# Seven accumulators of one pool for the main products and the shared work, in the place of four and three

## The chip, the cores and the metric

The kernel runs on one core of a Trainium2 chip. Its time is the device time of one execution in microseconds (us); the figure given for the kernel is the median of several runs. About 0.2% (1.4 us) is what a measurement of this kernel can tell from no change.

## What is computed

Three steps follow each other: attention that is read from a small state in both directions, a gated product (GLU) with a norm in front, and a mixture of experts over 32 soft slots.

```
# x: 8 x 8 x 512 x 64, state: 8 x 8 x 32 x 64
xread = softmax(scale * x @ state.T) @ state          # 512 rows of each batch and head
sread = softmax(scale * state @ x.T) @ x              # 32 rows of each batch and head
x = concat([xread, sread], 2) -> 4608 tokens x 512    # 8 heads x 64 side by side

xn = x / sqrt(mean(x * x) + 1e-6) * rms_g
h = silu(xn @ w_gate) * (xn @ w_val)                  # 512 -> 1536; weights arrive as float64
x = h @ w_out                                         # 1536 -> 512

logits = x @ phi                                      # 32 slots: 8 experts of 4
d = softmax over tokens(logits); c = softmax over slots(logits)
slot_out[e] = relu((d.T @ x)[e] @ w1[e]) @ w2[e]      # 512 -> 1024 -> 512
out = c @ slot_out
```

## The kernel before

A batch's 512 read rows are one group g of four tiles t of 128 tokens; the rows that the state reads form a last, smaller group. d_ff is cut into three chunks c of 512. A **unit** is one (g, c, t). In each unit TensorE (PE) makes the gate product of the tile (six matmuls of 128 x 512 into one accumulator, `mm<-wp,A` in the rows), ScalarE (ACT) takes its silu (L471), PE transposes an earlier unit's h (L109, `misc<-ident,h`), PE makes the value product (six more matmuls), VectorE (DVE) multiplies the two (L479, `h<-mm,rinv,sg`), and the logits of an earlier tile are added up (`lg<-hT,wphi`). Twelve units make a stage of one group.

The weights of the main products are not the raw ones: since attention's read is linear in the state, `sw` first multiplies the state's rows by the gate or value weights of a chunk (`misc<-w,stTg`). One call fills two accumulators, one for each half of the state's partitions (64 of the 128), with eight small matmuls each as the trace counts them; ACT copies each accumulator, rounded (L442), and DVE subtracts that from it for the rest (L443). The plan calls `sw` twice in a row, for gate and value, so four accumulators are filled one after another.

All else on PE goes through the same helper: scores (`misc<-xT,stT`), transposes (`sT`, `a`, `srd`), the product e2T (`misc<-xn,e2T`), the block product `misc<-bd,A`, the slots' inputs (`misc<-h,ET`), and, in the first part, `wphi_part`, which multiplies w_out by phi: per chunk two products `misc<-wo,phis`, gathered by DVE (L632 copy, L635 add, tile `wpp`), then `misc<-r,wpp`.

A plan written by hand says in which unit and slot each of these runs. The framework's scheduler makes from it one fixed instruction order per engine, and may pull a main matmul ahead into a gap where an accumulator is free by its reckoning. An engine runs its own list strictly in order. The accumulators lie in PSUM, which has eight banks of 128 x 512 float32:

- `mmps()` (L79): the main products' tiles, tag `mm`, four buffers. `keep_warm` (L106) and the products at the end take theirs here too.
- `misc()` (L82): all shared tiles, tag `misc`, three buffers.
- one bank for the logits, later for the experts' output (`lg`, `so`).

A tile waits until the tile that held its buffer before has been read for the last time. In `sw` the fourth tile of four takes the bank of the first.

The float64 weights come as bits by SyncE's (SP's) queue and are converted by ACT (L184, L187), DVE (L200, L204, L208) and GpSimd (POOL, L212). At about 97 to 116 us the last ones of the first stages are being made, among them w_out's (`wo`).

Of the kernel before, what the change touches and what calls it, by code (L numbers as in the profile page):

```python
# [8 lines left out]
F32 = mybir.dt.float32  # L9
# [11 lines left out]
def kernel(  # L21
# [17 lines left out]
    B, P, H, NT, D = x_n.shape  # L39
    S = P * NT  # L40
    NS = 32
    DM = H * D
# [10 lines left out]
    big = ctx.enter_context(tc.tile_pool(name="big", bufs=1))  # L53
    psp = ctx.enter_context(tc.tile_pool(name="psp", bufs=1, space=PSUM))
# [20 lines left out]
    def small(name, shape, bufs=1, dt=F32):  # L75
        return sm.tile(shape, dt, tag=name, bufs=bufs, name=name)

    def mmps():
        return psp.tile([P, 512], F32, tag="mm", bufs=4, name="mm")  # L79

    def misc():
        return psp.tile([P, 512], F32, tag="misc", bufs=3, name="misc")  # L82

    def mm(o, lhsT, rhs, start=True, stop=True):
        nc.tensor.matmul(out=o, lhsT=lhsT, rhs=rhs, start=start, stop=stop)  # L85

# [1 line left out]
    ident = small("ident", [P, P])  # L88
    make_identity(nc, ident)
    r32 = small("r32", [P, 32])  # L90
# [5 lines left out]
    rs_magic = small("rs_magic", [P, NT], dt=I32)  # L96
    nc.vector.memset(rs_magic.bitcast(F32), RS_MAGIC)

    # Bits of float64's high word, read as float32: the least and greatest that float32 holds.
    EXP_LO, EXP_HI = 2.0 ** -15, 122879.984375  # L100

    def keep_warm(n):
        """Products that nobody reads, so that a short wait doesn't slow the array's clock."""
        ps = mmps()
        for _ in range(n):
            tc.keep_in_program_order(nc.tensor.matmul(out=ps[:, :P], lhsT=ident, rhs=ident, start=True, stop=True))  # L106
# [1 line left out]
    def transpose(o, i):  # L108
        nc.tensor.transpose(o, i, ident)  # L109

# [1 line left out]
    XN, T = {}, {}  # L112

    def load_xt(b):
# [7 lines left out]
    def load_xn(b):  # L122
# [7 lines left out]
    phis = asmall("phis", [P, 4, NSLOT])  # L130
    nc.scalar.dma_start(out=phis, in_=phi)

# [1 line left out]
    dram = ctx.enter_context(tc.tile_pool(name="dram", bufs=1, space=bass.MemoryType.DRAM))  # L134
    w_out32 = dram.tile([DFF, DM], F32, name="w_out32")
    bits = {
        0: w_gate.bitcast(I32), 1: w_val.bitcast(I32), 2: w_out_t.bitcast(I32),
        3: w_out.bitcast(I32),
    }
# [81 lines left out]
                )  # L221


# [1 line left out]
    def att_g(b):  # L225
        stTg = small("stTg", [P, P], bufs=3)
        ins = nc.gpsimd.tensor_tensor(
# [173 lines left out]
    RINV = {}  # L401

    def rinv_from(g, ss, n):
        """(ss / DM + 1e-6) ** -0.5, by Newton's steps from the halved exponent."""
        y = small("rinv", [P, NT], bufs=3)[:, :n]
        v = small("rv", [P, NT])[:, :n]
        a = small("ra", [P, NT])[:, :n]
        i = small("ri", [P, NT], dt=I32)[:, :n]
        nc.vector.tensor_scalar(
            out=v, in0=ss, scalar1=1.0 / DM, scalar2=1e-6, op0=ALU.mult, op1=ALU.add  # L410
        )
        nc.vector.tensor_scalar(  # L412
            out=i, in0=v.bitcast(I32), scalar1=1, scalar2=-1,
            op0=ALU.logical_shift_right, op1=ALU.bitwise_xor,
        )
        nc.gpsimd.tensor_tensor(out=y.bitcast(I32), in0=i, in1=rs_magic[:, :n], op=ALU.add)  # L416
        for _ in range(3):
            nc.vector.tensor_tensor(out=a, in0=y, in1=y, op=ALU.mult)
            nc.vector.scalar_tensor_tensor(
                out=a, in0=a, scalar=-0.5, in1=v, op0=ALU.mult, op1=ALU.mult  # L420
            )
            nc.vector.scalar_tensor_tensor(
                out=y, in0=a, scalar=1.5, in1=y, op0=ALU.add, op1=ALU.mult
            )
        RINV[g] = y

# [1 line left out]
    WP = {}  # L428

    def sw(b, c, gv):  # L430
# [14 lines left out]
            )  # L445
        WP[b, c, gv] = t

# [1 line left out]
    HH, HT, LGP = {}, {}, {}  # L449
    xsg_t = {}  # L450
    wphi = small("wphi", [P, NF, 32])
# [56 lines left out]
                stop=(c == NC - 1),  # L508
            )

# [1 line left out]
    sacc = small("sacc", [P, 1])  # L512
    mrun = small("mrun", [P, 1])
    Q = {}
# [103 lines left out]
            out=v, in0=v, in1=cs[:, :n].unsqueeze(2).to_broadcast([P, n, 32]), op=ALU.mult  # L618
        )

# [1 line left out]
    wphi_done, WPP = set(), {}  # L622

    def wphi_part(c, j):
        """phi' @ w_out' for half of the d_model rows of a 512-wide chunk; j = 1 ends the chunk."""
        wt = WOT.pop((c, j))
        ps = misc()
        for k in range(2):
            mm(ps[32 * k : 32 * k + 32, :], phis[:, 2 * j + k, :], wt[:, k, :])
        if j == 0:  # L630
            WPP[c] = k2("wpp")
            nc.vector.tensor_copy(WPP[c][:64], ps[:64])  # L632
            return
        wp = WPP.pop(c)
        nc.vector.tensor_tensor(out=wp[:64], in0=ps[:64], in1=wp[:64], op=ALU.add)  # L635
        ps = misc()
        for q in range(4):
            mm(ps[:, 32 * q : 32 * q + 32], wp[:64, q * P : (q + 1) * P], r32[:64])
        nc.vector.tensor_copy(
            wphi[:, 4 * c : 4 * c + 4, :], ps[:, :P].rearrange("p (q s) -> p q s", q=4)  # L640
        )
        wphi_done.add(c)

# [1 line left out]
    def sread_prep():  # L645
        xg = k8("xg").rearrange("p a f -> p (a f)")[:, : 4 * B * NS].rearrange(
            "p (k n) -> p k n", k=4
# [23 lines left out]
    WH = {}  # L671

    def w_split(gv, c):
        """The weights' chunk in two float32r parts."""
        w = W.pop((gv, c))
        h, l = k8("wh", F32R), k8("wl", F32R)
        for k in range(4):
            nc.scalar.copy(h[:, k, :], w[:, k, :])
            nc.vector.tensor_tensor(
                out=l[:, k, :], in0=w[:, k, :], in1=h[:, k, :].bitcast(F32), op=ALU.subtract  # L680
            )
        WH[gv, c] = h, l

# [1 line left out]
    EW = {}  # L685
    loads = []
    for c in range(NC):
# [10 lines left out]
    ew_home, ew_free = {}, []  # L698

    def prefetch(n, home=None):  # L700
        """Start the next n loads, in slots of `big` (home None) or of the experts' pool."""
        for _ in range(n):
            if not loads:
                return
            k = loads.pop()
            if home is None:
                t = k8("ew")
            else:
                t = home.tile([P, 4, 512], F32, tag="ew", bufs=4, name="ew_" + "_".join(map(str, k)))
            if k[0] == "wo":  # L710
                src = w_out32[k[1] * 512 : (k[1] + 1) * 512, :].rearrange("(k p) d -> p k d", p=P)
            elif k[0] == "w1":
                src = w1[k[1], :, k[2] * 512 : (k[2] + 1) * 512].rearrange("(k p) f -> p k f", p=P)
            else:
                src = w2[k[1], k[2] * 512 : (k[2] + 1) * 512, :].rearrange("(k p) d -> p k d", p=P)
            nc.sync.dma_start(out=t, in_=src)
            EW[k], ew_home[k] = t, home
# [6 lines left out]
        while ew_free:  # L724
            prefetch(1, ew_free.pop(0))

# [1 line left out]
    def conv1(n=1):  # L728
        wconv(n)
        if len(to_load) > 6 and (to_load[-1][0] < 2 or len(RAW) < 3):  # L730
# [39 lines left out]
        rinv_from(0, T[0, "ss"], NT)  # L770

    pinned.append(1)
# [1 line left out]
    def rinv(b):  # L774
        rinv_from(b, T[b, "ss"], NT)

# [22 lines left out]
    for s, units in enumerate(stages):  # L799
# [65 lines left out]
            at(16, 1, att_a4, 2)  # L865
        else:
            g = s
            o = 4 if s == 1 else 0  # the first unit's place in the usual twelve
            if s == 1:
                at(0, 1, conv1)  # L870
                at(0, 2, wphi_part, 2, 1)
# [38 lines left out]
        for u, (g, c, t) in enumerate(units):  # L910
# [5 lines left out]
            ps = main_mm(g, c, t, 0)  # L916
# [40 lines left out]
    for u, (c, gv) in enumerate(halves):  # L957
# [3 lines left out]
        for t in range(2):  # L961
            ps = main_mm(gs, c, t, gv)
# [30 lines left out]
        prefetch(PU[u])  # L993
    assert not plan

# [1 line left out]
    h_T(*pend[0])  # L997
    lg_mm(*pend[0])
    post1(gs)
# [21 lines left out]
    for c in range(NC):  # L1021
        ps = mmps()
# [5 lines left out]
    ps = misc()  # L1028
# [27 lines left out]
    ps = misc()  # L1056
    for k in range(4):
        mm(ps[:, 32 * k : 32 * k + 32], sip[:, k * P : (k + 1) * P], r32)
    # each expert's inputs of its own slots, zero in the others'
    for e in range(NE):  # L1060
        es = slice(4 * e, 4 * e + 4)
        nc.vector.tensor_tensor(
# [8 lines left out]
    so_ps = psp.tile([P, 512], F32, tag="lg", bufs=1, name="so")  # L1071
# [7 lines left out]
    HP = {}  # L1079

    def expert_in(p):
        """The first products of two experts: slots of one have zeros in the other."""
        for j in range(2):
            ps = mmps()
            for i in range(2):
                e = 2 * p + i
                wt = take(("w1", e, j))
                for k in range(4):
                    mm(
                        ps[32 * k : 32 * k + 32, :], sinE[e][:, k, :], wt[:, k, :],  # L1090
                        start=(i == 0), stop=(i == 1),
                    )
            HP[p, j] = hp1[:, 2 * (p % 2) + j, :]
            (nc.scalar.copy if j else nc.vector.tensor_copy)(HP[p, j], ps)
# [26 lines left out]
                    )  # L1121

    def out_prep():
        """Group 0's weights of the slots, in two parts, each four times."""
        ch = k8("ch", F32R)[:, 0, :P].rearrange("p (t s) -> p t s", s=32)
        cs = k8("cs")[:, :2, :].rearrange("p i (t q s) -> p i t q s", t=NT, q=4)
        cr = k8("csT", F32R)
        nc.gpsimd.tensor_copy(ch, c_all[:, :NT, :])
        for q in range(4):
            nc.gpsimd.tensor_copy(cs[:, 0, :, q, :], ch.bitcast(F32))  # L1130
            nc.gpsimd.tensor_tensor(
                out=cs[:, 1, :, q, :], in0=c_all[:, :NT, :], in1=ch.bitcast(F32), op=ALU.subtract
            )
        return cs, cr
# [76 lines left out]
    c_turn(1)  # L1211
    expert_out(NPAIR - 1)

    # so_ps still has the four parts of each slot's sum; group 0 takes it as it is
    s4 = k8("s4", F32R)
    s4_h, s4_l = s4[:, 0, :], s4[:, 1, :]
    nc.scalar.copy(s4_h, so_ps)
# [16 lines left out]
    ps = misc()  # L1234
# [4 lines left out]
    so_h, so = so2[:, 0, :], so2[:, 1, :]  # L1239
# [64 lines left out]
```

## Time and profile before

| | |
|---|---|
| time, median of 3 runs | 690.22 us (689.71 to 690.36) |
| span of the profiled execution | 691.4 us |
| PE busy | 640.3 us (93%) |
| VectorE busy | 407.7 us (59%) |
| ScalarE busy | 388.9 us (56%) |
| chain that ended last | PE 75%, DVE 7%, ACT 5% |
| one stage in the middle | 63.8 us (283.8 to 347.6), PE busy 62.25 |

PE is close to always busy, so the page's shares say little; what matters is what PE does in its busy time and which waits stand between. In a timeline a row is a run of like matmuls: start, length, what, how many, and in brackets the idle time ahead of it with what ended it.

### The profile page before, as it was taken

How to read it: one execution, taken by the hardware profiler on the slowest of the kernel's cores; microseconds unless marked ns; L12 is line 12 of the kernel's file. 1: busy time of each engine (PE TensorE's matmuls, PEld its weight loads, DVE VectorE, ACT ScalarE, POOL GpSimd, SP SyncE). 2: the span in 40 equal slices, each digit the busy share in tenths (PEclk: the TensorE clock that was granted, in tenths of full speed). 3: DMA queues.
4: the chain of work that ended last, by engine and by line, in shares of the span. 5: the costliest groups of instructions: out<-in, count | busy, mean ns of one | idle time of the engine just before them, and what ended most of it. 6: DMA issues, size and time to landing. Idle time of an engine off the chain costs nothing.

```text
span 691.4 us, 11529 instructions
## 1 busy us (share of the span) xinstructions
PE 640.3 (93%) x4560; PEld 410.6 (59%) x4560; DVE 407.7 (59%) x852; ACT 388.9 (56%) x632; POOL 129.1 (19%) x158
## 2 busy tenths in 40 slices
PE   6789988999989999999999999999999999999980
PEld 4346646456555766566676658665666676753350
DVE  6979996762687457554835673575455355342160
ACT  5477943754776459546764765496446366311170
POOL 2634554230032101110201021011000000002430
PEclk9799998999999999999999999999999999999995
DMA  9940246031042011203110320020081307999957
GB/s 349 404 193 2 101 152 236 1 129 63 1 156 96 5 47 77 96 5 122 45 53 1 122 92 1 19 105 31 1 309 58 122 1 257 326 334 382 344 186 331
DMA packets 33581, 92.55 MB, mean 134 GB/s; under 512 B 1912, under 2 KB 4088, under 8 KB 30712
## 3 DMA queue, kind: packets, MB, share of 16 engines
q1 hardware_dynamic: 33240, 91.76, 36.3%
q8 instruction: 36, 0.59, 0.4%
q14 instruction: 17, 0.14, 0.1%
q10 hardware_dynamic: 288, 0.07, 0.0%
HBM read 79.76 MB, written 12.06 MB: 133 GB/s over the span
## 4 chain that ended last, share of the span: by engine, by line
PE 75%; DVE 7%; ACT 5%; issue 1%; POOL 0%; DVEq 0%; ACTq 0%
PE mm L85 42%; PE misc L85 17%; PE misc L109 10%; PE lg L85 3%; PE so L85 2%; DVE wp L443 1%; DVE h L479 1%; ACT wp L442 1%; ACT L471 1%; DVE wo L200 1%; ACT sg L471 1%; DVE wo L208 1%; DVE rm L272 1%; ACT sT L285 0%; DVE wo L204 0%
## 5 line engine op out<-in xcount | busy, mean ns | idle before, releaser
L85 PE MATMUL mm<-wp,A 128*128 128x512 f32 x1152 | 304.9, 405 | 0.4 <-DVE h L479 0.4
L85 PEld LDWEIGHTS mm<-wp,A 128*128 128x128 f32 x1152 | 207.3, 189 | 64.1 <-issue 24.5
L479 DVE SCALAR_TENSOR_TENSOR h<-mm,rinv,sg 128x512 f32<-128x512 f32 x102 | 76.1, 747 | 131.1 <-PE mm L85 93.6
L471 ACT ACTIVATE sg<-mm,rinv 128x512 f32<-128x512 f32 x102 | 70.2, 690 | 81.0 <-PE mm L85 78.0
L85 PE MATMUL misc<-w,stTg 64*32 64x512 f32 x768 | 81.7, 618 | 17.6 <-DVE wp L443 7.5
L442 ACT CAST wp<-misc 128x512 fp32r<-128x512 f32 x96 | 51.7, 591 | 65.2 <-PE misc L85 63.1
L443 DVE TENSOR_TENSOR wp<-misc,wp 128x512 fp32r<-128x512 f32 x96 | 61.8, 682 | 26.6 <-ACT wp L442 26.1
L109 PE MATMUL misc<-ident,h 128*128 128x128 f32 x408 | 61.3, 277 | 1.9 <-DVE h L479 0.7
L490 ACT COPY hT<-misc 128x512 f32<-128x512 f32 x86 | 49.2, 580 | 24.6 <-PE misc L109 20.5
L109 PEld LDWEIGHTS misc<-ident,h 128*128 128x128 f32 x408 | 50.1, 142 | 18.2 <-DVE wp L443 3.3
L85 PEld LDWEIGHTS misc<-w,stTg 64*32 64x32 f32 x768 | 15.5, 106 | 67.7 <-issue 22.1
L308 POOL TENSOR_TENSOR a<-a,asum 128x1024 f32<-128x1024 f32 x7 | 13.4, 1917 | 132.4 <-issue 84.8
L471 ACT ACT_TABLE_LOAD x28 | 35.9, 1283 | 3.7 <-PE mm L85 3.2
L416 POOL TENSOR_TENSOR rinv<-ri,rs_magic 128x4 int32<-128x4 int32 (+1 forms) x9 | 1.8, 198 | 173.2 <-DVE ri L412 173.2
L397 ACT ACTIVATE misc<-misc 128x512 f32<-128x512 f32 x32 | 18.7, 585 | 26.9 <-PE misc L85 18.8
L212 POOL TENSOR_TENSOR w<-w,raw 128x512 int32<-128x512 int32 x20 | 28.1, 1418 | 27.6 <-ACT wp L442 7.2
L85 PE MATMUL mm<-wh,xsg 128*128 128x512 f32 x96 | 31.7, 399 | 0.0
L85 PE MATMUL misc<-bd,A 128*128 128x256 f32 x192 | 29.6, 292 | 1.5 <-DVE A L380 1.5
L212 POOL TENSOR_TENSOR wo<-wo,raw 128x512 int32<-128x512 int32 x18 | 24.8, 1387 | 32.7 <-DVE wo L208 23.3
L85 PE MATMUL lg<-hT,wphi 128*32 128x512 f32 (+1 forms) x216 | 27.4, 577 | 1.5 <-ACT hT L490 1.5
L85 PEld LDWEIGHTS misc<-bd,A 128*128 128x128 f32 x192 | 25.5, 191 | 5.1 <-DVE A L380 2.2
L85 PE MATMUL misc<-h,ET 128*32 128x512 f32 x204 | 26.4, 596 | 0.0
(196 smaller groups left out, 831.8 us busy)
## 6 DMA issues: line engine op xcount, KB each, us to landing
ew<-in_w_dram SPq DMA_DIRECT2D x27, 1024.0 KB, 8.1
xT<-in_x_t_dram SPq DMA_DIRECT2D x8, 1024.0 KB, 5.5
xn<-in_x_n_dram SPq DMA_DIRECT2D x8, 1024.0 KB, 7.7
raw<-in_w_val_dram SPq DMA_DIRECT2D x6, 1024.0 KB, 16.6
raw<-in_w_out_dram SPq DMA_DIRECT2D x6, 1024.0 KB, 5.0
out_dram<-ob SPq DMA_DIRECT2D x6, 1024.0 KB, 12.1
ew_w<-in_w_dram SPq DMA_DIRECT2D x5, 1024.0 KB, 10.4
raw<-in_w_gate_dram SPq DMA_DIRECT2D x4, 1024.0 KB, 14.2
```

The costliest lines, as they stand in the source:

```text
L85: nc.tensor.matmul(out=o, lhsT=lhsT, rhs=rhs, start=start, stop=stop)
L109: nc.tensor.transpose(o, i, ident)
L200: nc.vector.tensor_scalar(out=dst[:, h], in0=dst[:, h], scalar1=EXP_LO, scalar2=EXP_HI, op0=ALU.max, op1=ALU.min,)
L208: nc.vector.scalar_tensor_tensor(out=a[:, h], in0=hi[:, h], scalar=-0x40000000, in1=a[:, h], op0=ALU.bitwise_and, op1=ALU.bitwise_or,)
L212: nc.gpsimd.tensor_tensor(out=a[:, h], in0=a[:, h], in1=rnd[:, h], op=ALU.add)
L308: (eng or nc.gpsimd).tensor_tensor(out=a3, in0=a3, in1=asum.unsqueeze(2).to_broadcast([P, 32, 32]), op=ALU.mult)
L397: nc.scalar.activation(out=ps, in_=ps, func=AF.Square, accum_out=T[b, "ss"][:, t : t + 1])
L442: nc.scalar.copy(t[:, r, 0, :], ps)
L443: nc.vector.tensor_tensor(out=t[:, r, 1, :], in0=ps, in1=t[:, r, 0, :].bitcast(F32), op=ALU.subtract)
L471: nc.scalar.activation(out=sg, in_=ps, func=AF.Silu, scale=RINV[g][:, t : t + 1])
L479: nc.vector.scalar_tensor_tensor(out=HH[g, c][:, t, :], in0=ps, scalar=RINV[g][:, t : t + 1], in1=sg, op0=ALU.mult, op1=ALU.mult,)
L490: (nc.vector.tensor_copy if on_dve else nc.scalar.copy)(HT[g, c][:, :, t * P : (t + 1) * P], ps.rearrange("p (q n) -> p q n", q=4))
```

## The change

The two helpers take their tiles from one tag with seven buffers. No instruction is added or taken away; the rest of the diff blanks comments and docstrings.

```diff
     def mmps():
-        return psp.tile([P, 512], F32, tag="mm", bufs=4, name="mm")
+        return psp.tile([P, 512], F32, tag="ps", bufs=7, name="mm")
 
     def misc():
-        return psp.tile([P, 512], F32, tag="misc", bufs=3, name="misc")
+        return psp.tile([P, 512], F32, tag="ps", bufs=7, name="misc")
```

The number of banks is the same, but a tile's buffer is now that of the tile seven allocations earlier, whichever of the two helpers made that. The scheduler's order moves with it. In what follows the counts are those of the program (a matmul of `misc<-w,stTg` or `lg`, in full float32, is two in the trace).

PE in a stage in the middle, around the two calls of `sw` (`w_696` and `w_776` are the gate and value weights, `wp_3112` and `wp_3127` the products' weights that are in use; - is before, + after):

```order
+L85 MATMUL mm<-wp_3127,A_2755 128x512 x6
 L85 MATMUL lg<-hT_3158,wphi 32x512 x4
 L85 MATMUL misc<-w_696,stTg 32x512 x8
 L85 MATMUL misc<-w_776,stTg 32x512 x8
-L109 MATMUL misc<-ident,sT 128x128 x4
-L85 MATMUL mm<-wp_3112,A_2755 128x512
-L109 MATMUL misc<-ident,sT 128x128 x4
-L85 MATMUL mm<-wp_3112,A_2755 128x512 x5
+L109 MATMUL misc<-ident,sT 128x128 x8
+L85 MATMUL mm<-wp_3112,A_2755 128x512 x6
```

The four tiles of `sw` stand together in both; the value product that stood farther ahead now stands right before the logits, and the transposes behind are no longer split by a main matmul.

PE at about 97 to 116 us of the first stages, before (`wp_734` to `wp_906` are main products, `wo_828` and `wo_884` two quarters of w_out, `xn_938` the next batch's rows, loaded just then):

```order
L85 MATMUL mm<-wp_869,A_255 128x512 x6
L85 MATMUL misc<-wo_828,phis 32x512 x2
L85 MATMUL mm<-wp_906,A_255 128x512 x6
L85 MATMUL mm<-wp_869,A_255 128x512 x6
...
L85 MATMUL mm<-wp_869,A_255 128x512 x4
L85 MATMUL misc<-xn_938,e2T 32x64 x32
L85 MATMUL misc<-wo_884,phis 32x512 x2
L85 MATMUL mm<-wp_869,A_255 128x512 x2
L85 MATMUL mm<-wp_906,A_255 128x512 x5
L85 MATMUL misc<-r_75,wpp 128x32 x4
```

The same place after:

```order
L85 MATMUL mm<-wp_734,A_255 128x512 x6
L85 MATMUL mm<-wp_869,A_255 128x512 x6
L85 MATMUL misc<-wo_828,phis 32x512 x2
L85 MATMUL misc<-xn_938,e2T 32x64 x32
L85 MATMUL mm<-wp_906,A_255 128x512 x6
L85 MATMUL misc<-wo_884,phis 32x512 x2
L85 MATMUL misc<-r_75,wpp 128x32 x4
```

From `wp_734` to `misc<-r_75,wpp` there are 53 main matmuls before and 18 after; the other 35 now stand behind that product.

PE where w_out's next chunk is multiplied (about 126 to 131 us), before, and then after:

```order
L85 MATMUL lg<-hT_1048,wphi 32x512 x4
L85 MATMUL misc<-wo_954,phis 32x512 x2
L85 MATMUL mm<-wp_1056,A_456 128x512 x5
L85 MATMUL mm<-wp_1108,A_456 128x512 x4
L85 MATMUL misc<-r_75,wpp 128x32 x4
```

```order
L85 MATMUL lg<-hT_1048,wphi 32x512 x4
L85 MATMUL misc<-wo_954,phis 32x512 x2
L85 MATMUL misc<-r_75,wpp 128x32 x4
L85 MATMUL mm<-wp_869,A_255 128x512 x6
L109 MATMUL misc<-ident,h_817 128x128 x8
```

Nine main matmuls that stood between the products with phi and the one that needs DVE's sum of them are gone from there. The third chunk (`wo_1123`) changes in the same way, with eight.

## Rows read from the trace of the kernel before

**Rows 1.** The page, part 1 (busy, share, instructions) and the granted clock in 40 slices:

```profile
PE 640.3 (93%) x4560; PEld 410.6 (59%) x4560; DVE 407.7 (59%) x852; ACT 388.9 (56%) x632; POOL 129.1 (19%) x158
...
PEclk9799998999999999999999999999999999999995
```

**Rows 2.** Who PE waited for: us in total, times, longest:

```profile
PE misc L85 <- DVE wp L443: 7.9, 14, 0.6
...
PE misc L85 <- DVE e2T L318: 3.1, 1, 3.1
```

**Rows 3.** Timeline of PE, one stage in the middle: start, length, work, count, idle ahead:

```profile
345.08 1.92 PE L85 MATMUL misc<-w,stTg 64*32 64x512 f32 x24
347.57 1.06 PE L85 MATMUL misc<-w,stTg 64*32 64x512 f32 x8 [0.57 <-DVE wp L443]
348.57 0.66 PE L109 MATMUL misc<-ident,sT 128*128 128x128 f32 x4
...
389.60 1.91 PE L85 MATMUL misc<-w,stTg 64*32 64x512 f32 x22
391.44 1.65 PE L85 MATMUL mm<-wp,A 128*128 128x512 f32 x6
```

**Rows 4.** Timelines of DVE and ACT behind the first of these bursts:

```profile
346.83 1.89 DVE L443 TENSOR_TENSOR wp<-misc,wp 128x512 fp32r<-128x512 f32 x3 [1.45 <-ACT wp L442]
...
346.21 1.56 ACT L442 CAST wp<-misc 128x512 fp32r<-128x512 f32 x3 [3.23 <-PE misc L85]
```

**Rows 5.** Timeline of PE, 180 to 204 us, the rows with a wait:

```profile
181.08 0.66 PE L109 MATMUL misc<-ident,h 128*128 128x128 f32 x4 [0.62 <-ACT sT L253]
...
191.52 0.66 PE L109 MATMUL misc<-ident,h 128*128 128x128 f32 x4 [0.55 <-DVE acc L596]
192.95 1.09 PE L109 MATMUL misc<-ident,sT 128*128 128x128 f32 x8 [0.78 <-DVE xsT L350]
```

**Rows 6.** Timeline of PE, 94 to 120 us:

```profile
97.17 4.13 PE L85 MATMUL mm<-wp,A 128*128 128x512 f32 x12
...
102.57 8.02 PE L85 MATMUL mm<-wp,A 128*128 128x512 f32 x34
110.53 1.10 PE L85 MATMUL misc<-xn,e2T 128*32 128x64 f32 x64
111.44 1.03 PE L85 MATMUL misc<-wo,phis 128*32 128x512 f32 x4
112.40 1.89 PE L85 MATMUL mm<-wp,A 128*128 128x512 f32 x7
116.02 1.39 PE L85 MATMUL misc<-r,wpp 64*128 64x32 f32 x8 [1.73 <-DVE wpp L635]
```

**Rows 7.** What this place waits for: SP's issue, its landing time, DVE's sum:

```profile
101.99 0.46 SPq L126 DMA_DIRECT2D xn<-in_x_n_dram  x1
...
DMA to landing us min/median/max: 7.1/7.1/7.1
...
115.29 0.67 DVE L635 TENSOR_TENSOR wpp<-misc,wpp 64x512 f32<-64x512 f32 x1
```

**Rows 8.** Windows: stretch, its length, busy of PE, PEld, DVE, ACT, POOL, clock, DMA share, GB/s:

```profile
116.00:165.00 49.00, 48.82 (x326) 27.65 (x329) 29.50 (x59) 30.27 (x48) 12.13 (x11) 0.93 0.22 79
...
118.00:120.00 2.00, 2.00 (x16) 1.35 (x22) 0.15 (x1) 1.02 (x2) 0.00 (x0) 0.50 0.00 0
...
538.60:595.00 56.40, 56.38 (x298) 41.91 (x299) 29.28 (x55) 32.58 (x56) 0.00 (x0) 1.00 0.43 150
595.00:650.00 55.00, 53.42 (x405) 26.43 (x407) 16.33 (x58) 8.65 (x20) 9.21 (x26) 1.00 1.00 356
```

**Rows 9.** Timeline of PE and DVE where w_out's second chunk is multiplied:

```profile
127.65 2.56 PE L85 MATMUL mm<-wp,A 128*128 128x512 f32 x9
130.31 1.07 PE L85 MATMUL misc<-r,wpp 64*128 64x32 f32 x8
...
129.59 0.67 DVE L635 TENSOR_TENSOR wpp<-misc,wpp 64x512 f32<-64x512 f32 x1
```

## The prediction, made before the changed kernel was run

> **What bounds the kernel now.** I read the page first: PE is busy for 640.3 of 691.4 us, and its clock is high in nearly every slice [rows 1]. So the time is PE's list of instructions plus its waits, and a change that moves no arithmetic can only act through waits, through how tightly PE's own work packs, and through the clock. The list of PE's waits comes second: the largest entry, 14 waits of at most 0.6 us, is for DVE's L443, the last reader of an accumulator of sw [rows 2]. The timeline of a stage shows what such a wait is: three accumulators are filled in one run of 24 matmuls, then the fourth starts late, since it needs the first one's bank [rows 3]. Thirteen of the 14 are this pattern, between 201 and 539 us; one is at 38 us. Last come the first 165 us, where PE waits for data and not for banks, and there I compare the order of instructions.
>
> The profiled span is 691.4 us and the median of the runs 690.22, so I sum against the span and take 1.2 us off at the end.
>
> **The bursts of sw.** What the profile calls idle is 0.57 us a burst, 13 x 0.57 = 7.4 us. That is a lower bound, because the idle time is not all that the wait costs. The fourth tile alone, eight matmuls, takes from 347.57 to 348.57, 1.00 us. In the other burst 22 matmuls, almost three tiles and without a wait, take from 389.60 to 391.44, 1.84 us [rows 3]. Tiles of the two halves of the state's rows run side by side on PE, and a tile that waits for its bank loses its partner. Four tiles with banks of their own are two pairs, and I price them at the 1.84 us of the 22 matmuls. The stalled burst took 348.57 - 345.08 = 3.49 us. So a burst saves 3.49 - 1.84 = 1.65 us, and 13 save **21.5 us**. I take this value, since it rests on the same work without the wait, and keep 7.4 as the other end.
>
> The Trainium skill, in "TensorEngine Tiling (Array Packing)", section "Gotcha 1: PSUM Pressure", says that row tiles run into different PSUM banks and may not use one bank at once, so that a bank is the price of running side by side. The rows agree in that 22 matmuls take 1.84 us and 8 alone 1.00 us; by this rule the gain is 21.5 us rather than 7.4, and the time 678 rather than 692.
>
> Does seven really free the burst? The readers of three tiles take 1.56 us on ACT and 1.89 us on DVE [rows 4], so four take about 2.5 us on DVE, from the end of the first pair on. In the new order a tile's bank comes back seven tiles later. Behind the four of sw stand two tiles of transposes and a main product, and before them a main product and others, so from one use to the next lie at least about 3 us of PE's work (four tiles 1.84 and a main product of six matmuls, about 1.4 by the rate below). That covers 2.5 us, narrowly where DVE is late.
>
> Between 165 and 202 us three more waits for banks go: 0.62 + 0.55 + 0.78 = **1.95 us** [rows 5].
>
> **The first stages.** Here the change costs. Before, the scheduler had four banks for main products alone and pulled 35 main matmuls ahead of work that waits for data; now they stand behind it. At 102.57 PE has done the same in both (12 main matmuls and the first products with phi). Then before has 34 main matmuls up to 110.53 [rows 6]. After comes xn, whose load SP issues at 101.99 and which lands 7.1 us later, at 109.1 [rows 7]: PE waits 6.5 us. Then xn's products (0.91), six main matmuls (1.4), the second products with phi (0.96): 112.4. Then misc<-r,wpp, which needs DVE's L635. That ends at 115.96 in before, held by the conversions of w_out ahead of it on DVE, and nothing in the change moves these: PE waits 3.6 us more, against 1.73 before. At 116.02 both kernels start the same product and 35 matmuls are still to do, at 7.96 / 34 = 0.234 us each [rows 6]: **8.2 us**. From 116 to 165 us PE is busy for 48.82 of 49 us in before [rows 8], so nothing gives this back. Bounds: 0, if DVE or the load come early by as much, and 12 if they come late by 4.
>
> The clock adds to it. In before the wait until 116.02 is followed by a stretch at a granted clock of 0.50, the lower level of 1.2 GHz [rows 8]. After an idle time of 6.5 us I expect the same from about 109 on. At half speed the 3.3 us of work there take about 6.5 and end at 115.6; L635 then ends behind them, at about 116.4 to 117. I take **+1 us**; -3 if the low stretch that before has behind 116 falls away, +3.5 if it comes a second time.
>
> The second and third chunk of w_out: before had nine main matmuls (2.56 us) between the products with phi and the one that needs their sum, and the sum on DVE (0.67 us, ending 0.05 before) lay beside them [rows 9]. After has none, so PE waits for the sum: 0.67 plus the handover and whatever DVE has in hand, about 1.1 us at each of two places, **+2.2 us**. Bounds 0 and twice 2.56, 5.1: what the removed cover held.
>
> From 25 to 92 us the order falls back to the plan's in the same way, and PE comes a few us later to single products. I cost this at nothing: its cover is the wait of 3.1 us that ends at 94.5 [rows 2], named by a bank (e2T), but behind it stands the conversion of the last gate weights, which the change doesn't move. If that cover is gone it costs up to 3 us; if only the bank held PE there, it gains up to 0.7.
>
> **Later moves.** In the stages the slots' inputs move ahead of a value product and the multiply behind three adds on DVE; DVE is 59% busy, and PE doesn't come back to that tile for a whole unit. Costed at nothing; 0 to 0.3 us a stage. At the end the loads of the experts' weights fill the DMA engines (1.00 from 595 to 650, against 0.43 ahead of it [rows 8]). They start when PE's progress frees their buffers, so an earlier PE starts them earlier, and the gain is carried over; up to 5 us of it could be lost there.
>
> **Sum:** -21.5 - 1.95 + 8.2 + 1 + 2.2 = -12.05. 691.4 - 12.05 - 1.2 = **678.2 us**, called 678.
>
> **Rivals.**
> - *The first stages give it back.* Either the data come sooner than I think, or PE's later work swallows the deficit (main matmuls that before left for 165 to 202 us pack without waits). Then 8.2 + 1 + 2.2 shrink to about 2, and the time is 690.2 - 23.4 + 2 = 669. For it: the banks were scarce there too [rows 5]. Against it: PE's 48.82 of 49 us ahead of that [rows 8].
> - *The readers bound the burst.* If a burst can't be shorter than DVE's 2.5 us for four tiles [rows 4], it saves 3.49 - 2.5 = 1.0 us and 13 save 13: 690.2 - 13 - 1.95 + 11.4 = 687. With only the shown idle, 7.4, it is 692. Against it: no tile right behind the burst needs these banks. The skill's same page, section "PSUM Bottleneck", has the rule that packing speeds PE but not the emptying of PSUM, which then may bound; by it, 687.
> - *Slower: the shared ring couples the main products to slow readers.* A main product's bank came back four main products later, 4 x 1.4 us or more of PE's work; now any late reader of a transpose or a score tile seven tiles back holds it. The price is one wait for each of the 204 main tiles. It turns the gain of 12 us into none from 12 / 204 = 0.06 us each; at 0.1 us it gives 690.2 - 12 + 20 = 698. For it: DVE and ACT have queues in which such a reader stands behind others. Against it: the 3 us above.
> - *No effect.* The banks were not what held the fourth tile, or another wait takes each one's place: 690.
>
> **How the numbers follow.** Forecast 678 with 674 to 683 around it: 0.52. Given back, 669: 0.20. Readers bound, 687 (692 at its end): 0.12. Coupled ring, 692 or more: 0.09. No effect: 0.07. Measured against the 0.2% that can be told from no change, faster is the first two and most of the third, 0.82; the same 0.07; slower 0.11. The range reaches from 664, a little under the second case, to 691, the end of the third; it leaves out the coupled ring and what lies under 664.
>
> **What would show it.** Right: in the stages no wait for L443, bursts of 32 matmuls in about 1.85 us, and a stage of 63.8 us about 3.3 us shorter (two bursts of four tiles in it stalled); between 102 and 116 a wait of about 6.5 us for xn's load and one of 2 to 4 for L635, a low clock behind the first; and PE's work at 165 us about 11 us later than before. Wrong: waits of main matmuls for readers of misc tiles, bursts over 2.5 us, or no wait for xn at all.

## The result and the profile after

The changed kernel takes 700.5 us (699.73 to 702.2, four runs) against 690.29 us of the kernel before: ratio 1.0145, interval 1.0123 to 1.0167. It is slower, and outside the range. The profiled executions, from which the rows come, differ by less, 698.8 against 691.4 us: a span is 1.8 us shorter than the time of the same execution (after's profiled one took 700.58 us), so before's was one of about 693 us, some 3 us over its median. Where these 3 us went can be seen, since the run e2_pin_squares below has the banks and PE's order of before up to 499 us. In it PE waits 0.38 us ahead of the first `misc<-r,wpp` (1.73 in [rows 6]), the granted clock is 1.00 from 116 to 122 us (0.50 from 118 to 120 in [rows 8]), and the logits that before's trace has at 163.44 start at 160.60:

```profile
115.81 1.07 PE L85 MATMUL misc<-r,wpp 64*128 64x32 f32 x8 [0.38 <-DVE wpp L637]
```

The page of after, part 1 and the granted clock, as in [rows 1]:

```profile
PE 627.7 (90%) x4560; PEld 413.6 (59%) x4560; DVE 409.2 (59%) x852; ACT 387.6 (55%) x632; POOL 128.4 (18%) x158
...
PEclk9598998999999999999999999999889999999995
```

PE is busy for 12.6 us less and the span is 7.4 us longer: work packs better, and waits have grown by more. The list of PE's waits in after, as in [rows 2] (total, times, longest):

```profile
PE misc L85 <- DMA xn<-in_x_n_dram: 8.9, 1, 8.9
PE misc L574 <- ACT E L555: 6.1, 7, 1.9
PE misc L85 <- POOL w L212: 5.8, 3, 4.6
PE misc L109 <- POOL a L308: 5.7, 1, 5.7
PE misc L85 <- DVE sq L653: 4.6, 1, 4.6
PE misc L85 <- DVE wpp L635: 3.6, 3, 2.0
```

The wait for L443, the largest of before, is gone. Of those in its place the prediction had xn and wpp; E (the transposes of E and L, L574) and sq (the squares for the state's rows) it had not. The wait for `a` (L308), 0.8 us in before, lies in the first 92 us; that for `w` (L212) was there before, with 6.5 us. A stage in before, where E's transposes don't wait, and then in after, as in [rows 3]:

```profile
335.68 0.32 PE L574 MATMUL misc<-ident,E 128*128 128x128 f32 x1
```

```profile
339.94 0.33 PE L574 MATMUL misc<-ident,E 128*128 128x128 f32 x1 [0.75 <-ACT E L555]
...
350.79 1.95 PE L85 MATMUL misc<-w,stTg 64*32 64x512 f32 x32
352.67 1.09 PE L109 MATMUL misc<-ident,sT 128*128 128x128 f32 x8
```

The burst of four tiles takes 352.67 - 350.79 = 1.88 us (3.49 before), close to the 1.84 forecast. But E's transposes, which in before stood behind four more main matmuls, wait 0.75 us for ACT. The third of the stage in which they lie takes 20.68 us (329.11 to 349.79, from logits to logits) where before takes 19.27 for the same matmuls (324.84 to 344.11), and the whole stage 61.72 (288.07 to 349.79) where before takes 63.76 (280.35 to 344.11): 2.0 us shorter, not the 3.3 of the forecast.

About 100 to 120 us in after, as in [rows 6]:

```profile
103.55 1.05 PE L85 MATMUL misc<-wo,phis 128*32 128x512 f32 x4
113.52 1.94 PE L85 MATMUL misc<-xn,e2T 128*32 128x64 f32 x64 [8.91 <-DMA xn<-in_x_n_dram]
115.39 2.09 PE L85 MATMUL mm<-wp,A 128*128 128x512 f32 x6
117.41 1.05 PE L85 MATMUL misc<-wo,phis 128*32 128x512 f32 x4
119.27 1.08 PE L85 MATMUL misc<-r,wpp 64*128 64x32 f32 x8 [0.81 <-DVE wpp L635]
```

This is the forecast mechanism with a longer wait, 8.9 us instead of 6.5. SP issues the load at 104.44 here, 101.99 before, but PE too comes about 2 us later; the rest is the load itself, which lands 8.9 us after its issue and not 7.1:

```profile
103.94 0.46 SPq L118 DMA_DIRECT2D xT<-in_x_t_dram  x1
104.44 0.43 SPq L126 DMA_DIRECT2D xn<-in_x_n_dram  x1
...
DMA to landing us min/median/max: 8.9/8.9/8.9
```

The load of xT, issued 0.5 us ahead of it, is not there in before; that it is the reason is not shown.

The squares, in before and then in after:

```profile
498.56 1.06 PE L85 MATMUL misc<-w,stTg 64*32 64x512 f32 x8 [0.57 <-DVE wp L443]
499.55 3.70 PE L85 MATMUL mm<-wp,A 128*128 128x512 f32 x15
503.09 1.84 PE L85 MATMUL misc<-ones,sq 128*128 128x1 f32 x16
```

```profile
496.17 1.95 PE L85 MATMUL misc<-w,stTg 64*32 64x512 f32 x32
502.72 3.58 PE L85 MATMUL misc<-ones,sq 128*128 128x1 f32 x16 [4.61 <-DVE sq L653]
506.16 2.91 PE L85 MATMUL mm<-wp,A 128*128 128x512 f32 x6
508.86 1.05 PE L109 MATMUL misc<-ident,h 128*128 128x128 f32 x4
509.57 4.29 PE L85 MATMUL mm<-wp,A 128*128 128x512 f32 x12
```

Fifteen main matmuls that covered DVE's squares stand behind them now. PE waits 4.61 us; then the same work runs slowly. The window of after (length, busy of PE, PEld, DVE, ACT, POOL, clock, DMA share, GB/s):

```profile
506.00:510.00 4.00, 4.00 (x13) 3.31 (x13) 1.95 (x12) 0.69 (x1) 0.20 (x1) 0.50 1.05 398
```

The granted clock is 0.50, the lower of its two levels (1.2 GHz), and the six main matmuls take 508.86 - 506.16 = 2.70 us, about twice 1.4.

Where the time went shows when both kernels start the same logits, with the same matmuls behind them (up to two of them at 217 us). The difference is the ledger of the whole run:

| logits in before at | in after at | after is behind by |
|---|---|---|
| 163.44 | 173.41 | 9.97 |
| 217.05 | 226.33 | 9.28 |
| 495.07 | 495.17 | 0.10 |
| 514.32 | 522.02 | 7.70 |
| 584.46 | 591.67 | 7.21 |
| end of the span, 691.4 | 698.8 | 7.4 |

The first stages lose 10 us, the stages win 9.2 back, the squares cost 7.6 at one stroke. The 2.8 us by which before's profiled execution was late all lie ahead of the first row: against e2_pin_squares the first stages lose 12.8 us, and the end is 10.2 behind, as the medians are.

### The profile page after: what moved, and what is told of

Read it like the earlier page. It is cut to its first block, busy times and chain, and to the rows that moved or that the text cites. A ratio compares the mean times of both kernels' runs of the same rounds, so it can differ in the third digit from the quotient of the medians.

```text
span 698.8 us, 11517 instructions
## 1 busy us (share of the span) xinstructions
PE 627.7 (90%) x4560; PEld 413.6 (59%) x4560; DVE 409.2 (59%) x852; ACT 387.6 (55%) x632; POOL 128.4 (18%) x158
## 4 chain that ended last, share of the span: by engine, by line
PE 73%; DVE 12%; ACT 7%; DMA 2%; issue 2%; POOL 0%; SPq 0%; ACTq 0%; DVEq 0%
PE mm L85 41%; PE misc L85 17%; PE misc L109 9%; PE lg L85 4%; PE so L85 2%; DVE w L200 2%; DVE w L208 2%; DVE wp L443 1%; DVE h L479 1%; DMA xn<-in_x_n_dram 1%; DVE w L204 1%; ACT sg L471 1%; ACT L471 1%; ACT L555 1%; DMA raw_t<-in_w_gate_dram 1%
## 5 line engine op out<-in xcount | busy, mean ns | idle before, releaser
L85 PE MATMUL mm<-wp,A 128*128 128x512 f32 x1152 | 308.1, 409 | 1.0 <-ACT sT L253 1.0
L85 PEld LDWEIGHTS mm<-wp,A 128*128 128x128 f32 x1152 | 209.5, 192 | 68.7 <-issue 14.6
L443 DVE TENSOR_TENSOR wp<-misc,wp 128x512 fp32r<-128x512 f32 x96 | 61.2, 684 | 24.8 <-ACT wp L442 24.2
L85 PE MATMUL misc<-w,stTg 64*32 64x512 f32 x768 | 62.1, 614 | 8.9 <-POOL w L212 5.8
L85 PEld LDWEIGHTS misc<-w,stTg 64*32 64x32 f32 x768 | 12.5, 107 | 45.6 <-issue 29.9
L308 POOL TENSOR_TENSOR a<-a,asum 128x1024 f32<-128x1024 f32 x7 | 13.4, 1916 | 133.9 <-issue 79.6
L85 PE MATMUL misc<-bd,A 128*128 128x256 f32 x192 | 31.3, 305 | 3.1 <-DVE A L380 3.1
L212 POOL TENSOR_TENSOR w<-w,raw 128x512 int32<-128x512 int32 x20 | 27.7, 1394 | 29.2 <-DVE w L208 8.4
L212 POOL TENSOR_TENSOR wo<-wo,raw 128x512 int32<-128x512 int32 x18 | 24.7, 1389 | 36.1 <-DVE wo L208 36.1
L85 PEld LDWEIGHTS misc<-bd,A 128*128 128x128 f32 x192 | 27.0, 202 | 6.1 <-DVE A L380 3.4
## 6 DMA issues: line engine op xcount, KB each, us to landing
raw<-in_w_val_dram SPq DMA_DIRECT2D x6, 1024.0 KB, 16.5
```

The source lines that it names most:

```text
L212: nc.gpsimd.tensor_tensor(out=a[:, h], in0=a[:, h], in1=rnd[:, h], op=ALU.add)
L308: (eng or nc.gpsimd).tensor_tensor(out=a3, in0=a3, in1=asum.unsqueeze(2).to_broadcast([P, 32, 32]), op=ALU.mult)
L443: nc.vector.tensor_tensor(out=t[:, r, 1, :], in0=ps, in1=t[:, r, 0, :].bitcast(F32), op=ALU.subtract)
```

## The experiments

The **order theory**: the bursts gain what was forecast, and the loss is that main products no longer stand ahead of shared work that waits for data, at three places: xn and wpp, E and L, the squares. The **ring theory**, its rival: main products and shared tiles in one ring of banks hold each other up. The first runs take the two apart on the kernel before, whose banks stay as they are.

**One place of the order alone.** `keep_in_program_order` puts an instruction behind the one that the program has ahead of it on its engine. For the squares (run e2_pin_squares), at the main product behind them; `mm` now returns its instruction:

```diff
-            mm(ps, A[:, r, la, ts], wp[:, r, lw, :], start=(i == 0), stop=(i == 5))
+            ins = mm(ps, A[:, r, la, ts], wp[:, r, lw, :], start=(i == 0), stop=(i == 5))
+            if i == 0 and (g, c, t, gv) == (B - 2, 2, 1, 0):
+                tc.keep_in_program_order(ins)
```

> The kernel before with one main product held back: the one that follows the sum of squares (misc<-ones,sq at about 500 us) in the program may not be issued ahead of it. All else, banks too, stays. Order theory: PE waits about 4.6 us for DVE's squares as in the changed kernel, then runs at the low clock for a few us, and 15 main matmuls are done later: 6 to 8 us more, 697 us. Ring theory (these waits come from the shared banks): no change, 690 us.

Measured: 698.1 us, ratio 1.0113 (1.0096 to 1.0131), 7.9 us more. PE in this run:

```profile
499.89 3.54 PE L85 MATMUL misc<-ones,sq 128*128 128x1 f32 x16 [3.09 <-DVE sq L655]
503.29 2.91 PE L85 MATMUL mm<-wp,A 128*128 128x512 f32 x6
506.00 1.05 PE L109 MATMUL misc<-ident,h 128*128 128x128 f32 x4
```

With the banks of before the same wait and the same slow stretch appear. The wait is shorter than the 4.6 us expected, since the burst ahead of it still stalls and PE comes later. So these 7 to 8 us are order, not banks.

For xn and wpp (e3_pin_xn) the condition is `(g, c, t, gv) in ((0, 2, 0, 1), (0, 2, 1, 0))`:

> The kernel before with two main products held back at about 102 us: they may not be issued ahead of misc<-xn,e2T and misc<-r,wpp. Banks as before. Order theory: PE waits 6 to 9 us for xn's load and then for DVE's sum, 35 main matmuls are done later (8.2 us), and little of it comes back: 8 to 11 us more, 700 us. Ring theory: no change, 690 us. If the stages behind 165 us had slack for it: 692 to 694.

Measured: 701.48 us, ratio 1.0163 (1.0145 to 1.0182), 11.3 us more, at the upper end of what was expected. The rows answer to [rows 6]:

```profile
110.74 1.94 PE L85 MATMUL misc<-xn,e2T 128*32 128x64 f32 x64 [5.64 <-DVE wo L204]
...
118.19 1.08 PE L85 MATMUL misc<-r,wpp 64*128 64x32 f32 x8 [2.51 <-DVE wpp L637]
```

(The trace names DVE for the first wait; behind it stands xn's load, issued at 103.56 and landed 7.0 us later.) The two waits are 8.15 us in all, and nothing behind 165 us has slack for them: the run is 11.8 us behind e2_pin_squares at the logits of 163.44 (172.38 against 160.60) and still 11.7 at those of 367.53 (376.49 against 364.75).

For E and L (e4_pin_E), post3 sets a flag for groups 1 to 6, and the next main product is held back:

```diff
+            if i == 0 and T.pop("pin", False):
+                tc.keep_in_program_order(ins)
...
         Q[g, "ET"] = ET
+        T["pin"] = g in range(1, 7)
```

> The kernel before with the main product that follows the transposes of E and L held back behind them in the groups 1 to 6. Banks as before. Order theory: PE waits 0.75 us for E from ACT in each of five stages and loses about 1 us in each: 4 to 5 us more, 695 us. Ring theory: no change, 690 us.

Measured: 698.7 us, ratio 1.0121 (1.0104 to 1.0138), 8.5 us more, almost twice the expected. The wait is what was expected:

```profile
336.45 0.33 PE L576 MATMUL misc<-ident,E 128*128 128x128 f32 x1 [0.77 <-ACT E L557]
...
342.52 1.92 PE L85 MATMUL misc<-h,ET 128*32 128x512 f32 x16
344.38 0.50 PE L85 MATMUL mm<-wp,A 128*128 128x512 f32 x1
344.81 1.07 PE L85 MATMUL misc<-h,ET 128*32 128x512 f32 x8
```

But a stage grew by 1.6 us (63.77 to 65.37 between the same logits; in after the same place costs 1.4), so the hold also moved what comes after, as the split of the slots' inputs shows. Which part of the rest is whose was not taken apart.

All three holds together (e12_pin_three):

> The kernel before with the three holds of e2_pin_squares, e3_pin_xn and e4_pin_E together: banks of before, order of the changed kernel at the three places. If the three costs add up: 690.2 + 7.9 + 11.3 + 8.5 = 718 us, and the 17 us between that and the changed kernel's 700.5 are what the shared banks give. If they overlap: 700 to 712 us.

Measured: 717.04 us, ratio 1.0376 (1.035 to 1.0401). The three costs add up (690.2 + 27.7 = 717.9). With the order of the changed kernel at these three places, the banks of before are 16.5 us slower than the shared pool (717.04 - 700.5). That is what the shared banks bring, with whatever else they move in the order, and the ring theory, by which they cost, has fallen.

**The same places mended in the changed kernel.** The squares (e7_shared_squares), with the products split off as `sread_rest`:

```diff
                 at(8, 2, sread_prep)
+                at(10, 1, sread_rest)
```

> The changed kernel (one pool of seven) with the eight products of the squares (misc<-ones,sq) moved a unit and a half behind DVE's part in the plan. Order theory: the wait of 4.6 us and the low clock behind it go, nothing else moves: 6.5 to 8 us off 700.5, 693 us. If the wait only hides another one that ends as late: 698 to 700.

Measured: 694.69 us (691.84 to 695.54), 5.8 us less. In the profiles the place itself gave 8.5 us (522.02 to 513.49 for the same logits), of which 1.6 went again by 585 us. E and L half a unit later (e8_shared_E_later):

```diff
-                at(u + 2, 2, post3, pg)
+                at(u + 3, 1, post3, pg)
```

> The changed kernel with the transposes of E and L moved half a unit later in the plan. Seven waits for E from ACT, 6.1 us as the list shows them, go. Order theory: 6 to 8 us off 700.5, 693 to 694.5 us. If PE only reaches the next wait earlier (the slots' inputs, which need E's transposes): 697 to 700 us.

Measured: 697.86 us, 2.6 us less, nearer to the second case. The waits for E fall to 2.4 us, and another takes their place:

```profile
340.65 0.27 PE L574 MATMUL misc<-ident,E 128*128 128x128 f32 x1
340.76 0.27 PE L575 MATMUL misc<-ident,L 128*128 128x128 f32 x1
340.79 3.01 PE L85 MATMUL mm<-wp,A 128*128 128x512 f32 x12
344.74 0.66 PE L109 MATMUL misc<-ident,h 128*128 128x128 f32 x4 [0.94 <-DVE h L479]
```

E's transposes wait no more, but a unit later h does: 0.94 us in each stage. So at this place E was not the last limit; the multiply of h was nearly as late, and a stage in the middle is as long as in after, 61.66 us (287.96 to 349.62) against 61.72. What the run won lies elsewhere: 1.0 us between the logits at 173.41 and 226.33 of after, and 1.3 at the squares, where the work up to the next logits takes 18.00 us and not 19.30. What holds the multiply was not measured apart.

The first stages (e9_shared_xn):

```diff
             at(12, 2, wphi_part, 0, 1)
+            at(13, 1, wphi_r, 0)
...
-            at(12, 1, att_b2, 1)
-            at(12, 2, att_b3, 1)
+            at(15, 1, att_b2, 1)
+            at(15, 2, att_b3, 1)
```

and the same for the other two chunks, wphi_r being the product misc<-r,wpp.

> The changed kernel (one pool of seven) with the first stages' plan changed: the product of xn (misc<-xn,e2T of the second batch) three units later, and each misc<-r,wpp half a unit behind the products with phi. Order theory: the wait of 8.9 us for xn's load goes, those for DVE's sum (3.6 us in three) shrink, and DVE's first sum now stands ahead of two conversions: 6 to 10 us off 700.5, 691 to 694 us. If the first stages are bound by the conversions on DVE and POOL anyway: 697 to 700 us.

Measured: 690.31 us, 10.2 us less, ratio to the kernel before 0.9993 (0.9977 to 1.0009). PE now runs almost through:

```profile
110.38 1.04 PE L85 MATMUL misc<-wo,phis 128*32 128x512 f32 x2 [0.20 <-POOL wo L212]
111.36 1.66 PE L85 MATMUL mm<-wp,A 128*128 128x512 f32 x6
112.85 1.03 PE L109 MATMUL misc<-ident,h 128*128 128x128 f32 x8
113.82 1.07 PE L85 MATMUL misc<-r,wpp 64*128 64x32 f32 x8
```

The product with r starts at 113.82, earlier than in before (116.02), since DVE's sum now stands ahead of most of its work for w_out's conversions and is done at 112.25 (115.96 in before). The prediction had taken it as given that they stand ahead of the sum; the plan can turn that round.

All three (e10_shared_three_mends):

> The changed kernel with all three places mended: the squares as in e7_shared_squares, E and L as in e8_shared_E_later, the first stages as in e9_shared_xn. Order theory: the three add up, 700.5 - 5.8 - 2.6 - (6 to 10) = 682 to 686 us, below the kernel before: then the shared pool by itself is a gain and the order made the loss. Ring theory: what is mended comes back at other waits and it stays above 692.

Measured: 681.63 us, ratio 0.9864 (0.9835 to 0.9893). 700.5 - 5.8 - 2.6 - 10.2 = 681.9: they add up again. One pool of seven is 8.9 us faster than the kernel before (690.54 us in the runs made beside it) once the plan keeps work that waits for data behind enough main products. Thirteen bursts at 1.8 us would be 23 us. A part of the difference is the wait for h, which this run still has seven times, 5.7 us in all; the rest was not taken apart.

**How many banks, and for whom.** Three and four, in two pools (e1_three_four):

```diff
-        return psp.tile([P, 512], F32, tag="mm", bufs=4, name="mm")
+        return psp.tile([P, 512], F32, tag="mm", bufs=3, name="mm")
-        return psp.tile([P, 512], F32, tag="misc", bufs=3, name="misc")
+        return psp.tile([P, 512], F32, tag="misc", bufs=4, name="misc")
```

> Two pools as before, but three banks for the main products and four for the shared tiles. Order theory (the bursts of sw gain some 21 us once four tiles have a bank each, and the loss of the shared pool comes from main products that no longer stand ahead of work that waits for data): here the order keeps the 15 main matmuls ahead of the sum of squares, the four ahead of the transposes of E and L, and 30 of the 35 at 102 to 116 us, so the bursts' gain is left almost alone: 690.3 - 21.5 + 1 to 3, about 671 us (667 to 676), bursts of 32 matmuls in 1.85 to 1.95 us. Ring theory (a burst gains little, since its readers bound it, or the gain is given back at the next tiles): 685 to 690 us.

Measured: 685.61 us, ratio 0.9936 (0.9919 to 0.9953): 14 us short of what was expected, at the rival's edge. The rows show a reason:

```profile
340.34 1.95 PE L85 MATMUL misc<-w,stTg 64*32 64x512 f32 x32
342.84 1.25 PE L109 MATMUL misc<-ident,sT 128*128 128x128 f32 x8 [0.55 <-DVE wp L443]
...
365.44 1.66 PE L85 MATMUL misc<-xT,stT 64*32 64x512 f32 x16 [0.55 <-DVE wp L443]
```

The burst is fast, and the next shared tile takes the wait over: it needs the bank of the burst's first tile. At the scores (xT) the packing is lost with it, 367.03 - 365.44 = 1.59 us for 16 matmuls instead of 1.00. The bursts' gain needs a bank for the tile behind them too, or other work there. That was tried next (e5_three_four_apart):

```diff
-                at(4, 2, att_b1, nb)
+                at(5, 1, att_b1, nb)
...
-                at(8 - o, 2, att_a3, nb)
+                at(9 - o, 1, att_a3, nb)
```

> Three and four banks as in e1_three_four, and the two shared steps that stand right behind a burst of sw (the transposes of sT for e2T, and the scores misc<-xT,stT) moved half a unit later in the plan, so that a main product stands between. In e1_three_four the four tiles of sw run without a wait, but the next shared tile takes the wait over: 0.55 us for L443 at sT and at xT, twice a stage, and the two tiles of the scores no longer run side by side. If the wait was only handed on to the next taker of a bank, a main product of 1.4 us in between covers it: 1.3 to 2 us a stage and the same in the stages ahead, 9 to 13 us off e1_three_four, 673 to 677 us. If it is handed on once more, to the transposes of h: 684 to 686 us.

Measured: 677.52 us, ratio 0.9799 (0.9781 to 0.9816), the fastest version seen: 8.1 us off e1, a little less than expected, so the handed-on wait was 8 of the 14 us that e1 fell short; the rest stays open. A main product now follows the burst, and by the time the shared tile comes the bank is free:

```profile
337.96 1.95 PE L85 MATMUL misc<-w,stTg 64*32 64x512 f32 x32
339.84 1.66 PE L85 MATMUL mm<-wp,A 128*128 128x512 f32 x6
341.33 0.60 PE L109 MATMUL misc<-ident,h 128*128 128x128 f32 x4
341.77 1.04 PE L109 MATMUL misc<-ident,sT 128*128 128x128 f32 x8
```

The plan's change alone, with four and three banks (e11_apart_alone):

> The kernel before (four and three banks) with the plan of e5_three_four_apart: sT's transposes and the scores half a unit later. With three banks for the shared tiles the fourth tile of sw still waits in each burst, so if banks and plan only work together this gives 0 to 4 us, 686 to 690 us. If the plan alone made the gain of e5: 678 to 681 us.

Measured: 691.74 us, ratio 1.0004 (0.9989 to 1.0018): no difference. The banks alone gave 4.6 us, the plan alone nothing, both together 12.6. And five banks for the shared tiles, two for the main products (e6_two_five):

> Two banks for the main products, five for the shared tiles; the order keeps the squares, E and L and most of the first stages as before. If the number of banks behind a burst decides and main products need no more than two: no wait at the tile behind the burst, 673 to 678 us. If two are too few, because a main product waits for the silu or the multiply of the one two before it, 0.1 us at each of 204 is 20 us: 690 us or more, with waits of mm for ACT L471 or DVE L479.

Measured: 694.65 us, ratio 1.0048 (1.0022 to 1.0075). The list of PE's waits of this run:

```profile
PE mm L85 <- ACT sg L471: 8.7, 9, 1.5
PE mm L85 <- DVE h L479: 8.0, 6, 3.6
```

With five banks no shared tile waits behind a burst: L443 stands in this list with 0.2 us, once. But two banks are too few for the main products: they wait for the silu and the multiply in single places, up to 3.6 us.

## Why the prediction was wrong

**The bursts: right.** A burst was to fall from 3.49 to 1.84 us and takes 1.88. Between the logits at 344.11 and 407.88 of before, and the same ones of after, the starts of `misc<-w,stTg` and `misc<-xT,stT` take 2.98 and 0.59 us less for two stalled bursts, 1.8 us each against the 1.65 forecast. The rule of the Trainium skill that the prediction set beside it ("TensorEngine Tiling (Array Packing)", section "Gotcha 1: PSUM Pressure") was on the right side: the gain is three times the 0.57 us of shown idle time. The rival that the readers bound the burst has fallen: they need about 2.5 us by the prediction's estimate, and the burst takes 1.88.

**Between 165 and 202 us: not as forecast.** The three waits went (1.95 us), and others of 1.0, 0.6 and 0.4 us came in their place, with one of 0.4 for hT and the first for E (0.76) behind them. Together with the burst that was freed there, after wins only 0.7 us from 163 to 217 us.

**The first stages: right in place, kind and nearly in size.** +11.4 was forecast; +9.97 was measured against before's trace and 12.8 against e2, whose execution is a usual one. e3 and e9 show the place from both sides, 11.3 and 10.2 us. Single terms were off and cancelled: the wait for xn was 8.9 and not 6.5 us, that for the first sum 0.8 and not 3.6, and those for the second and third 2.0 and 0.8 where 1.1 each was taken. The clock fell behind xn's wait as expected (0.50 from 113.50 to 115.40). But the low stretch that before's trace has behind 116 is not there in after (1.00 from 119.20 to 124.00): the case that the prediction priced at -3. It is not in e2 either, so it belonged to that one execution of before, and it hides 2.8 us of the loss in the +9.97. And "PE has done the same in both" holds for the work but not for the time: what before has done at 102.57 (e2 at 103.73), after has done at 104.61. That fits the change of order from 25 to 92 us, which the prediction put at nothing and at 3 us at most; the wait for `a` (L308) in it is 5.7 us and was 0.8.

**"Later moves", costed at nothing: the step that failed.** I had read the order of the stages and named the slots' inputs and a multiply, but not that the transposes of E and L had lost the four main matmuls in front of them, nor that the squares had lost their fifteen. The first costs 1.4 us in each stage of after and 8.5 when made on the kernel before; that moving E alone won 2.6 is no measure of it, since the wait passed to h. The second is worth 5.8 us when mended and 7.9 when made. I had looked for waits in the stages by banks alone, not by data. In the squares the wait is only 4.61 of the 7.6 us. From there to the next logits the same matmuls take 522.02 - 502.72 = 19.30 us, at first at the low clock, and took 514.32 - 499.55 = 14.77 in before: 4.53 more, and the freed burst takes 1.54 off.

The forecast laid out by the stretches of the ledger, with the thirteen bursts where they lie, shows where its 22 us went (the first stretch against e2, the others against before's trace):

| stretch of before, us | forecast | measured |
|---|---|---|
| to 163 | +11.4 | +12.8 |
| 163 to 217 | -3.6 | -0.7 |
| 217 to 495, stages with E and L | -14.9 | -9.2 |
| 495 to 514, the squares | -1.7 | +7.6 |
| 514 to the end | -3.3 | -0.3 |

The last stretch has a wait for E of 1.86 us as well; what else it lost was not taken apart.

So the mistake was not a size but a place. The prediction knew that the new order no longer lets main products stand ahead of work that waits for data, and priced that where the profile of before already showed PE near a wait. At the two other places before shows no wait at all, because the cover was complete (503.09 for the squares, 335.68 for E, both without idle time ahead). A wait that is fully covered leaves no row.

**The rivals.** "Slower" was given to a shared ring that makes main products wait for late readers. The list of waits holds little of the kind (1.0 us for sT L253 at 180 us, once; in e9 and e10 one of 1.4 us for L443), and e12 against the changed kernel says the reverse: the shared banks bring 16.5 us. Slower came out for another reason, one that the forecast had in it and had priced at one place of three; the chance it gave to slower was for a mechanism that the runs don't show.

## What to carry to other kernels

When two pools become one, read the new order for every place where independent work used to stand ahead of an instruction that waits for data, not only where the profile shows a wait: a cover that works shows none. Count the banks behind a burst as its tiles plus those of the shared step right after it (with four the step behind waited 0.55 us, with five it didn't), or put work from another pool there. And idle time at a bank wait understates its price where tiles run side by side: 0.57 us shown, 1.6 to 1.8 won.

## What the runs showed of the hardware

After the wait of 4.61 us the clock was at its lower level from 502.70 to 512.00 us, while PE was busy throughout, twice as long as the wait itself:

```profile
502.70:512.00 9.30, 9.28 (x32) 8.12 (x33) 3.05 (x13) 1.27 (x2) 0.20 (x1) 0.50 0.82 298
```

The same matmuls took 4.53 us longer, about as much again as the wait. In the kernel with the hold at the squares a wait of 3.09 us was followed by the same 2.70 us for six main matmuls (503.29 to 506.00, about 1.4 at the full clock), and the work up to the next logits took 18.81 us (499.89 to 518.70) and not 14.77, 4.04 more. So wait and low clock together cost 2.0 and 2.3 times the wait. That is no fixed factor: behind the wait of 8.91 us at 113.52 the low clock cost about 1.6 us (xn's products 1.87 and not 0.91, the six main matmuls 2.02 and not about 1.4), and from 117.40 on the granted clock is 1.00 again.
